# Load order at the start, block 1's inputs kept in SBUF, and outputs held back to stand beside scores, in a memory-augmented transformer with an MLP mixer

## The chip, the cores and the metric

The kernel runs on one core of a Trainium2 chip. The metric is the device time of one execution in microseconds (us), lower is better. A profile comes from one execution, in most runs one of those that are timed. Runs were made in jobs, each with its own runs of the kernel before: the first pair, then three jobs of experiments, of which the first two ran on one chip and the last on another.

Names of engines: PE is the tensor engine, PEld its weight loads, DVE the vector engine, ACT the scalar engine, POOL the gpsimd engine, SP the engine that issues most transfers.

## The reference, cut to what matters

```python
x = A_x                                   # 2048 tokens x 1024, bf16
xn = _layernorm(x)
return x + _A_ref(xn, mem0, Wq, Wk, Wv, Wo, 32) + _B_ref(xn, w1, w2, w3, w4)

# _A_ref: attention in 64 segments of 32 tokens, each with 8 memory rows, 32 heads of 128
#   scores = q k^T * scale; p = softmax(masked scores); o = (p v) Wo
#   the first 8 rows of o are the next segment's memory
# _B_ref: h = gelu(layernorm(x) @ w1); four column groups of h shifted by -1, +1, -2, +2 tokens
#   x1 = x + shifted @ w2; x1 + gelu(layernorm(x1) @ w3) @ w4
```

## The kernel before: the parts that matter

The kernel runs the mixer and the MLP first and the attention afterwards. Its matmul stream is written out by hand. Three places are touched by the change.

The start loads tiles of x (256 KB each) and quarters of w1 (512 KB each) on one queue, SP's. I call them x0, x1, ... and q0 to q3. The first tile is normalized on DVE, transposed on PE and copied by ACT; then 16 matmuls follow for each quarter of w1, as the quarters land.

```python
load_x(0)
load_x(1)
for c in range(4):
    nc.sync.dma_start(w1_sb[:, 2*c:2*c+2, :], w1_v[:, 2*c:2*c+2, :])
    if c == 1:
        load_x(2)
for n in range(3, 7):
    load_x(n)
...
norm_stats(0)
norm_stats(1, 0)          # first half of tile 1's statistics, ahead of tile 0's scaling on DVE
norm2_of(0)
tr(0, 0, True); tr(0, 1, True)
norm_stats(1, 1)
```

Attention works through 5 blocks of 12 to 14 segments. A block's tokens and memory rows, transposed, are gathered in `hTb`. Block 0's are filled straight into SBUF; those of blocks 1 to 4 are filled into a staging tile, written to DRAM, and read back later.

```python
if 1 <= hg < 5:
    hTs = abig.tile(...)                       # staging
    nc.gpsimd.memset(hTs[:], 0.0)
    fill(hTs, tl, lambda j, b=b: xT[:, j])     # DVE copies
    nc.gpsimd.dma_start(hT_d[b][:], hTs[:]...)
```

In attention the big projection matmuls are interrupted by small groups of four: scores (S) and outputs (O). `tick` runs after each projection and issues what is due. An output becomes due 10 us (12 in block 0) after its scores, on the kernel's own count of time. In between, P, the normalized scores, is made on ACT and DVE and transposed by a transfer on SP's queue.

```python
def tick(us, blocked=None):
    clock[0] += us
    load_some(1)
    done = set()
    for item in list(smalls):
        due, kind, fn = item
        if due <= clock[0] and kind != blocked and kind[0] not in done and not (kind[0] == "S" and flying[0] >= 5):
            smalls.remove(item)
            flying[0] += 1 if kind[0] == "S" else -1
            done.add(kind[0])
            clock[0] += fn()
...
smalls.append((clock[0] + (12.0 if gi_ == 0 else 10.0), ("O", gi_), o_item))
```

## Time and profile before

| what | value |
|---|---|
| time, median of the first 3 runs | 1512.88 us (1511.96 to 1513.14) |
| span of the profiled execution | 1511.0 us |
| PE busy | 1499.8 us |
| start of the matmuls of w1's third quarter | 11.32 us |
| first matmul of the attention's projections | 756.06 us |

From the page of the kernel before: the span, the busy time of the engines, the shares of the chain that ended last, and the three costliest PE groups (busy us, mean ns of one, idle us before them).

```profile
span 1511.0 us, 24305 instructions
PE 1499.8 (99%) x9778; PEld 804.0 (53%) x9850; DVE 544.6 (36%) x1136; ACT 504.6 (33%) x1144; POOL 178.9 (12%) x248
...
DMA packets 303539, 274.11 MB, mean 181 GB/s; under 512 B 153926, under 2 KB 270184, under 8 KB 303424
...
PE 98%; DMA 1%; issue 0%; SPq 0%; DVE 0%
...
L655 PE MATMUL ps<-hTb,wt 128*128 128x396 bf16 (+2 forms) x2528 | 495.9, 343 | 0.0
L594 PE MATMUL ps<-wt,xT 128*128 128x512 bf16 x1003 | 220.1, 379 | 1.1
L713 PE MATMUL pso<-wo_sb,oX 128*128 128x512 bf16 (+1 forms) x972 | 209.1, 372 | 1.1
```

PE is the limit. The idle 1.1 us of two groups fit missing records, not waits. The waits view of the kernel before, PE alone, in us in total, times, longest:

```profile
PE ps L307 <- DMA w_sb<-in_B_w_dram: 1.7, 3, 1.0
PE warm L334 <- DVE wz L328: 1.4, 1, 1.4
PE psO L694 <- DMA PT<-Pn: 0.5, 1, 0.5
```

Besides the warm-up there are three waits at the start for w1 and one for a transposed P. The timeline of PE at the start of the kernel before shows the three (start us, duration, engine, line, operation, operands, count, and in brackets the idle time before and what ended it). L307 is w1's matmuls, 16 for each quarter; L294 is the transposes.

```profile
6.53 0.96 PE L294 MATMUL ps<-c_ident_sb,xn 128*128 128x128 bf16 x8
7.96 1.07 PE L307 MATMUL ps<-xn2T,w_sb 128*128 128x128 bf16 x16 [0.47 <-DMA w_sb<-in_B_w_dram]
9.28 1.07 PE L307 MATMUL ps<-xn2T,w_sb 128*128 128x128 bf16 x16 [0.26 <-DMA w_sb<-in_B_w_dram]
11.32 1.07 PE L307 MATMUL ps<-xn2T,w_sb 128*128 128x128 bf16 x16 [0.97 <-DMA w_sb<-in_B_w_dram]
12.23 0.61 PE L294 MATMUL ps<-c_ident_sb,xn 128*128 128x128 bf16 x8
```

In attention, the timeline of PE of the kernel before shows what a pair of small groups costs: from 848.97 to 849.33 us, 0.36 us for eight matmuls of 99 columns, with no idle time on either side.

```profile
848.97 0.34 PE L694 MATMUL psO<-PT,V 99*128 99x99 bf16 x4
849.15 0.34 PE L670 MATMUL psS<-KT,QT 128*128 128x99 bf16 x4
849.33 0.84 PE L655 MATMUL ps<-hTb,wt 128*128 128x403 bf16 x4
```

A matmul's duration in the profile (343 ns in the group above) overlaps the next one's. What counts for the span is the distance between starts: 99 columns come to about 44 ns each, 396 columns to 167.5 ns.

### The profile page before, as it was taken

To read this page: it belongs to the slowest core of one execution; us is meant where nothing else is said; L and a number is where in the kernel's file an instruction comes from. 1 tells how busy PE (TensorE), PEld (TensorE's weight loads), DVE (VectorE), ACT (ScalarE), POOL (GpSimd) and SP (SyncE) were. 2 spreads that over 40 slices of the span, in tenths; PEclk is the share of its full clock that TensorE was granted. 3 is DMA by queue.
4 is the path that set the end of the run, shared out by engine and by line. 5 is a ranking of instruction groups with operands and counts; after the bars stand their busy time and mean duration, and the time that the engine had idled before them with its cause. 6 is when DMAs were issued, how large, how long until landed. Compare 5 with 4: busy or idle time off the path is not lost.

```text
span 1511.0 us, 24305 instructions
## 1 busy us (share of the span) xinstructions
PE 1499.8 (99%) x9778; PEld 804.0 (53%) x9850; DVE 544.6 (36%) x1136; ACT 504.6 (33%) x1144; POOL 178.9 (12%) x248
## 2 busy tenths in 40 slices
PE   9999999999999999999999999999999999999998
PEld 7844444445444444444456645664665455545555
DVE  8383230100020122222246624661564166516641
ACT  6533203013012011111156614650663266416630
POOL 5231020211111231100000000001000100010001
PEclk9999999999999999999999999999999999999999
DMA  8699752453345887632389957992998299918811
GB/s 292 150 265 315 228 168 89 146 202 104 137 149 151 203 261 258 218 121 82 128 216 257 244 128 171 245 252 69 245 243 206 71 227 224 219 60 199 216 49 51
DMA packets 303539, 274.11 MB, mean 181 GB/s; under 512 B 153926, under 2 KB 270184, under 8 KB 303424
## 3 DMA queue, kind: packets, MB, share of 16 engines
q1 hardware_dynamic: 281248, 189.92, 50.1%
q0 software_dynamic: 22032, 82.54, 15.9%
q8 instruction: 79, 1.29, 0.4%
q14 instruction: 36, 0.29, 0.1%
q10 hardware_dynamic: 144, 0.07, 0.0%
HBM read 190.93 MB, written 46.14 MB: 157 GB/s over the span
## 4 chain that ended last, share of the span: by engine, by line
PE 98%; DMA 1%; issue 0%; SPq 0%; DVE 0%
PE ps L655 30%; PE pso L713 15%; PE ps L594 15%; PE ps L536 13%; PE ps L562 13%; PE ps L394 4%; PE ps L317 3%; PE psO L694 2%; PE psS L670 2%; PE ps L849 1%; PE ps L486 1%; DMA w_sb<-in_B_w_dram 1%; DMA PT<-Pn 1%; PE gps L465 0%; PE ps L451 0%
## 5 line engine op out<-in xcount | busy, mean ns | idle before, releaser
L655 PE MATMUL ps<-hTb,wt 128*128 128x396 bf16 (+2 forms) x2528 | 495.9, 343 | 0.0
L655 PEld LDWEIGHTS <-wt 128*128 128x128 bf16 x2528 | 232.7, 98 | 164.9 <-DMA wt<-in_A_Wq_dram 0.4
L594 PE MATMUL ps<-wt,xT 128*128 128x512 bf16 x1003 | 220.1, 379 | 1.1
L713 PE MATMUL pso<-wo_sb,oX 128*128 128x512 bf16 (+1 forms) x972 | 209.1, 372 | 1.1
L536 PE MATMUL ps<-xn3T,w_sb 128*128 128x512 bf16 x896 | 196.2, 379 | 0.0
L562 PE MATMUL ps<-w_sb,h3T 128*128 128x512 bf16 x873 | 194.3, 379 | 1.2
L594 PEld LDWEIGHTS <-xT 128*128 128x128 bf16 x1024 | 100.1, 98 | 120.9
L537 ACT ACTIVATE h3T<-ps 128x512 bf16<-128x512 f32 x112 | 66.8, 597 | 290.4 <-PE ps L536 289.5
L713 PEld LDWEIGHTS <-oX 128*128 128x128 bf16 x992 | 96.0, 98 | 106.6
L657 ACT CAST KT<-ps 128x462 bf16<-128x462 f32 (+2 forms) x160 | 81.7, 511 | 190.0 <-PE ps L655 185.9
L562 PEld LDWEIGHTS <-h3T 128*128 128x128 bf16 x896 | 86.9, 98 | 103.4
L536 PEld LDWEIGHTS <-w_sb 128*128 128x128 bf16 x896 | 86.5, 98 | 102.1
L676 DVE TENSOR_REDUCE sums<-sm 99x4 f32<-99x396 f32 (+2 forms) x176 | 97.6, 555 | 112.9 <-ACT sm L674 112.9
L659 ACT ACTIVATE QT<-ps 128x462 bf16<-128x462 f32 (+2 forms) x160 | 83.8, 524 | 112.6 <-PE ps L655 98.7
L596 ACT CAST Vs<-ps 128x512 bf16<-128x512 f32 x64 | 37.4, 585 | 233.2 <-PE ps L594 175.0
L672 DVE TENSOR_TENSOR sm<-psS,c_mask_reg_sb 99x396 f32<-99x396 f32 x152 | 86.7, 570 | 74.6 <-PE psS L670 74.5
L674 ACT ACTIVATE sm<-sm 99x396 f32<-99x396 f32 (+2 forms) x176 | 92.7, 527 | 57.7 <-DVE sm L672 53.5
L600 DVE CAST Vs<-ps 128x512 bf16<-128x512 f32 x64 | 44.3, 692 | 170.0 <-PE ps L594 160.4
L682 DVE TENSOR_TENSOR Pn<-sm,rs 99x396 bf16<-99x396 f32 (+2 forms) x176 | 98.9, 562 | 7.2 <-DMA PT<-Pn 1.1
L720 POOL DMA_DIRECT2D out_dram<-ot x30 | 16.4, 545 | 699.4 <-DVE ot L719 693.5
L563 DVE TENSOR_TENSOR R<-ps,R 128x512 f32<-128x512 f32 x32 | 21.9, 690 | 180.1 <-PE ps L562 166.2
L719 DVE TENSOR_TENSOR ot<-pso,Rt 128x512 bf16<-128x512 f32 (+1 forms) x33 | 22.2, 675 | 168.5 <-PE pso L713 164.5
(122 smaller groups left out, 1063.0 us busy)
## 6 DMA issues: line engine op xcount, KB each, us to landing
wt<-in_A_Wq_dram SPq DMA_DIRECT2D x76, 512.0 KB
wt<-in_A_Wk_dram SPq DMA_DIRECT2D x76, 512.0 KB
wt<-in_A_Wv_dram POOLq DMA_DIRECT2D x24, 1024.0 KB, 6.9
V_scratch<-Vs SPq DMA_DIRECT2D x32, 512.0 KB
V<-V_scratch SPq DMA_DIRECT2D x40, 384.0 KB
R_scratch<-x POOLq DMA_DIRECT2D x16, 512.0 KB, 4.0
R<-R_scratch SPq DMA_DIRECT2D x16, 512.0 KB
R_scratch<-R POOLq DMA_DIRECT2D x16, 512.0 KB, 3.1
```

What stands on the lines that cost most here:

```text
L536: nc.tensor.matmul(ps[:].rearrange("p (n t) -> p n t", t=P), w3_sb[:, k, f * P:(f + 1) * P], xn3T[tb][:, :, k, :], start=(k == 0), stop=(k ...
L537: nc.scalar.activation(h3T[:, f, :], ps[:], ACTF.Gelu_apprx_tanh)
L562: nc.tensor.matmul(ps[:], h3T[:, f, j * P:(j + 1) * P], w4_sb[:, f, ch * 512:(ch + 1) * 512], start=(f == 0), stop=(f == FT - 1))
L594: nc.tensor.matmul(ps[:], xT[:, m4 * 4 + j, k, :], wv[:, k, :], start=(k == 0), stop=(k == KT - 1))
L655: nc.tensor.matmul(ps[:, :nb], w[:, k, hh * P:(hh + 1) * P], B["hT"][:, k, :nb], start=(k == 0), stop=(k == KT - 1))
L657: nc.scalar.copy(dst[:, hh, :], ps[:, :nb])
L659: nc.scalar.mul(dst[:, hh, :], ps[:, :nb], scale)
L672: nc.vector.tensor_tensor(sm[:T, :, :T], S3, t["mask"][:].unsqueeze(1).to_broadcast((T, 4, T)), op=ALU.add)
L674: nc.scalar.activation(e[:T, :, :T], sm[:T, :, :T], ACTF.Exp, scale=LN2)
L676: nc.vector.tensor_reduce(ss, e[:T, :, :T], axis=AX.X, op=ALU.add)
L682: nc.vector.tensor_tensor(Pn[:T, :, :T], e[:T, :, :T], rs[:T, :].unsqueeze(2).to_broadcast((T, 4, T)), op=ALU.mult)
L713: nc.tensor.matmul(self.ps[:, :self.w], self.oX[0][:, h, self.oX[1] + self.gl * P:self.oX[1] + (self.gl + 1) * P], wo_sb[:, h, self.cc], s ...
```

## The change

The intent: start w1's matmuls sooner, spare block 1's inputs the way through DRAM, and interrupt the projections less often, by letting an output wait (at most 2.5 us on the kernel's count) until the next scores go out.

```diff
-                    load_x(0)
-                    load_x(1)
+                    load_x(0)
                     for c in range(4):
                         nc.sync.dma_start(w1_sb[:, 2 * c:2 * c + 2, :], w1_v[:, 2 * c:2 * c + 2, :])
-                        if c == 1:
-                            load_x(2)
+                        if c < 2:
+                            load_x(1 + c)
...
                     norm_stats(0)
-                    norm_stats(1, 0)
                     norm2_of(0)
                     tr(0, 0, True)
                     tr(0, 1, True)
-                    norm_stats(1, 1)
+                    norm_stats(1)
...
-                if 1 <= hg < 5:
+                if hg < 2:
+                    tl, nb = tiles_of(hg)
+                    hTb01.append(early.tile([P, KT, 416 + 48 * hg], BF16, tag=f"hTb{hg}", name=f"hTb{hg}"))
+                    fill(hTb01[hg], tl, lambda j: xT[:, j])
+                elif hg < 5:
...
-            for item in list(smalls):
+            ready = [i for i in smalls if i[0] <= clock[0] and i[1] != blocked]
+            paired = any(k[0] == "S" for _, k, _ in ready) and flying[0] < 5 or not any(k[0] == "S" for _, k, _ in smalls)
+            for item in ready:
                 due, kind, fn = item
+                if kind[0] == "O" and not paired and clock[0] < due + 2.5:
+                    continue
```

More of the change, by code (lines that the diff above doesn't have):

```diff
@@ L112 @@
     xn_v = xn_d.rearrange("(n p) d -> p n d", p=P)
-    hT_d = {b: tc.dram_tile([P, KT * c], BF16, name=f"hT{b}_scratch") for b, c in ((1, 416), (2, 416), (3, 464), (4, 464))}
+    hT_d = {b: tc.dram_tile([P, KT * c], BF16, name=f"hT{b}_scratch") for b, c in ((2, 416), (3, 464), (4, 464))}
     V_d = tc.dram_tile([S, H * DH], BF16, name="V_scratch")
@@ L580 @@
             wo_sb = abig.tile([P, H, D], BF16)
+            hTb01 = []
             pns = [abig.tile([112, 4, P], BF16, name=f"Pn{i}") for i in range(3)]
@@ L618 @@
                         nc.sync.dma_start(w[:], src[:, :, 512:1024])
-                if hg == 0:
-                    tl, nb = tiles_of(0)
-                    hTb0 = early.tile([P, KT, 416], BF16, tag="hTb0")
-                    fill(hTb0, tl, lambda j: xT[:, j])
             vctx.close()
@@ L632, in block_setup @@
             ntok = sum(t["ntok"] for t in tl)
-            if b == 0:
-                hTb = hTb0
+            if b < 2:
+                hTb = hTb01[b]
             else:
```

## The prediction

> **What bounds the kernel now.** The tensor engine (PE) is busy 1499.8 of 1511.0 us (page, part 1), is 98% of the chain that ended last (part 4), at a granted clock of 1.00; the waits view gives PE only 1.7 us on w1's quarters at the start, 1.4 us before the warm-up and 0.5 us on a transposed P. Busy is not yet peak, so I took start-to-start distances from the trace. The Trainium skill ("TensorE: Matmul & The Clock Gate", section "Wait — 56ns, not 53.3ns?") gives N / 2.4 GHz plus about 2.5 ns for a warm matmul of N columns. The trace agrees almost everywhere: eight projections of 396 columns take 1.34 us, 167.5 ns each. Distances above that, leaving out those that fit a missing record, sum to about 4 us after the warm-up. So a change that removes no matmul can win some 4 us (0.3%).
>
> **Block 1's inputs in SBUF.** Removes one memset on POOL, one 0.85 MB write (near 559 us) and one read back (647 us, landed in 8.4 us, first used over 200 us later). PE waits for neither. Its ten DVE copies (0.18 to 0.36 us each) stay; they may move earlier, as block 0's did (DVE sat 11.3 us waiting for x's transposes near 485 to 497 us). That can delay evictions of the MLP's second product, but four PSUM tiles of 6.05 us each give slack. Gain on PE: 0.
>
> **x tiles between w1's quarters.** On one queue x0, x1, q0, q1, x2, q2 becomes x0, q0, x1, q1, x2, q2. q0 lands one x tile earlier (about 0.7 us), but q1 and q2 have the same bytes before them as before. The waits ending at 7.96 us (0.65 us), 9.28 us (0.42 us) and 11.32 us (1.14 us) are in series: the first shrinks, the next grows by as much, and PE still stands until q2 lands at 11.3 us. x1 lands later (near 7.9 us), so the second tile's normalized rows come near 11.2 us instead of 9.26 us, which the transposes at 12.2 us just allow. Gain 0, at worst a loss of 0.5 us.
>
> **Outputs held back.** Four score matmuls take 0.18 us on PE, as do four output matmuls, alone or as a pair (848.97 to 849.33 us), so interrupting the projections costs nothing measurable: 0 to 2 ns a change. Before, 73 of 176 output groups stand beside a score group in the trace; replaying the issue rule on paper gives about 145 after. Some 70 fewer interruptions are below 0.3 us. Outputs come up to 2.5 us later after their transposed P: the one 0.63 us wait at 799.4 us should go, perhaps 0.13 us at 1405 us. Scores keep their places.
>
> **Sum.** 1512.88 − 0.7 = about 1512.2 us; 8 times in 10 within 1510.4 to 1513.7. Faster by over 2%: 0.01; same: 0.98; slower: 0.01.
>
> **What would show it.** Right: PE busy within 2 us of 1499.8; part 5's means unchanged; waits for w1 again about 1.7 us, with the third quarter's matmuls starting near 11.3 us; about 145 output groups beside scores, still 0.18 us per group; no wait of outputs on P near 800 us; 1.7 MB less traffic. Wrong: third quarter's matmuls a microsecond earlier (the queue is not simply in order), groups shorter or longer in pairs, new PE waits for PSUM near 500 us or on P.
>
> **What would make it wrong.** A collision on the transposes' queue, copies placed so badly on DVE that PE runs out of PSUM tiles, or x1 landing so late that it holds the first transposes.

## The result, and the profile after

The changed kernel took 1510.90 us (median of 6 runs, 1510.73 to 1511.99), the kernel before in the same rounds and the earlier ones 1513.01 us (6 runs, 1511.96 to 1513.98). The ratio is 0.9988, with a 95% interval of 0.9975 to 1.0001. Ratios here are the mean time of one kernel's runs over that of the other's in the same rounds, so not quite the ratio of the medians. By the 2% measure the two are the same; the difference, about 2 us, is at the edge of what the runs separate, and it is the profile that tells what it is made of.

From the page of the changed kernel, the lines that answer to those shown before:

```profile
span 1509.0 us, 24273 instructions
PE 1499.1 (99%) x9778; PEld 804.6 (53%) x9850; DVE 544.6 (36%) x1136; ACT 504.0 (33%) x1144; POOL 175.0 (12%) x245
...
DMA packets 303251, 272.41 MB, mean 181 GB/s; under 512 B 153894, under 2 KB 270152, under 8 KB 303136
...
L654 PE MATMUL ps<-hTb,wt 128*128 128x396 bf16 (+2 forms) x2528 | 484.8, 342 | 0.0
L593 PE MATMUL ps<-wt,xT 128*128 128x512 bf16 x1003 | 220.1, 379 | 1.1
L712 PE MATMUL pso<-wo_sb,oX 128*128 128x512 bf16 (+1 forms) x972 | 208.5, 372 | 1.1
```

The number of matmuls and their mean durations are unchanged, and 1.70 MB of traffic are gone. The 11 us less on the projections are no saving. Before each break, the last projection's duration of 343 ns counts in full, though the next matmul starts 167 ns after it; with 72 breaks fewer (207 instead of 279 in the traces) an estimated 72 x 0.17 = 12 us of overlap are no longer counted to this group (e_outs below, which has the same 207 breaks, shows the same 484.8 us). PE as a whole is busy 0.7 us less. This is a trap in reading busy times group by group.

The waits of PE in the changed kernel, without the warm-up's 1.4 us:

```profile
PE ps L306 <- DMA w_sb<-in_B_w_dram: 0.3, 1, 0.3
PE ps L306 <- ACT xn2T L296: 0.2, 1, 0.2
PE psO L693 <- DMA PT<-Pn: 0.2, 1, 0.2
```

And its timeline of PE at the start (L306 is w1's matmuls):

```profile
7.45 1.95 PE L306 MATMUL ps<-xn2T,w_sb 128*128 128x128 bf16 x32 [0.24 <-ACT xn2T L296]
9.71 1.07 PE L306 MATMUL ps<-xn2T,w_sb 128*128 128x128 bf16 x16 [0.32 <-DMA w_sb<-in_B_w_dram]
10.62 0.61 PE L293 MATMUL ps<-c_ident_sb,xn 128*128 128x128 bf16 x8
11.08 1.07 PE L306 MATMUL ps<-xn2T,w_sb 128*128 128x128 bf16 x16
```

The first two quarters now run without a break, 32 matmuls from 7.45 us, and the third starts at 9.71 instead of 11.32 us. The mixer's second stage (its first matmul with w2) starts at 67.47 instead of 69.06 us: 1.59 us of the gain of 2.0 us in the span lie here. Everything from there to the attention takes equally long, 687.00 us in both.

The rest, 0.5 us, lies in attention. The stretch from its first projection to the last matmul takes 750.34 instead of 750.84 us. To see what it is made of, I set each PE start against the start before it plus N / 2.4 GHz + 2.5 ns (N is the number of columns; the formula is the one that the prediction cites), and called the excess before an output group a wait on P (these sums are a little larger than those of the waits view). That gives 0.79 us before and 0.52 us after, and a break of 0.19 us between projections at 791.9 us that is gone.

The DVE copies for block 1 were indeed moved ahead, from near 557 us to between 495.4 and 509.2 us. In the view of the tile `hTb` in the changed kernel, DVE's idle time for x's transposes is:

```profile
DMA xT<-xn_scratch: 17.2, 6
```

It was 11.3 us in 3 waits before. One eviction of the MLP's second product, at 509.22 us, had to stand behind them. No wait of PE came of it, as the prediction had argued.

### The profile page after: what moved, and what is told of

Read it like the earlier page. It is cut to its first block, busy times and chain, and to the rows that moved or that the text cites. A ratio compares the mean times of both kernels' runs of the same rounds, so it can differ in the third digit from the quotient of the medians.

```text
span 1509.0 us, 24273 instructions
## 1 busy us (share of the span) xinstructions
PE 1499.1 (99%) x9778; PEld 804.6 (53%) x9850; DVE 544.6 (36%) x1136; ACT 504.0 (33%) x1144; POOL 175.0 (12%) x245
## 2 busy tenths in 40 slices
DMA packets 303251, 272.41 MB, mean 181 GB/s; under 512 B 153894, under 2 KB 270152, under 8 KB 303136
## 4 chain that ended last, share of the span: by engine, by line
PE 98%; DMA 1%; issue 0%; SPq 0%; DVE 0%
PE ps L654 30%; PE pso L712 15%; PE ps L593 15%; PE ps L534 13%; PE ps L560 13%; PE ps L392 4%; PE ps L316 3%; PE psO L693 2%; PE psS L669 2%; PE ps L852 1%; PE ps L484 1%; DMA PT<-Pn 1%; PE gps L463 0%; PE ps L449 0%; DMA w_sb<-in_B_w_dram 0%
## 5 line engine op out<-in xcount | busy, mean ns | idle before, releaser
L654 PE MATMUL ps<-hTb,wt 128*128 128x396 bf16 (+2 forms) x2528 | 484.8, 342 | 0.0
L654 PEld LDWEIGHTS <-wt 128*128 128x128 bf16 x2528 | 236.8, 98 | 175.4
```

Source lines behind the costliest of these rows:

```text
L654: nc.tensor.matmul(ps[:, :nb], w[:, k, hh * P:(hh + 1) * P], B["hT"][:, k, :nb], start=(k == 0), stop=(k == KT - 1))
```

## The experiments

Two questions were open. Why does the third quarter land 1.6 us sooner, when the same bytes are ahead of it in the queue? And what, if anything, does the holding back of outputs gain? My theories: T, the order of the loads itself moves the landing; W, held outputs gain only because P has more time to land. Rivals: R, the start differs by chance; P, standing beside scores makes the groups cheaper for PE (this "rival P" has only its letter in common with the matrix P); A, less traffic helps. A second pair, X and Q, came up later and is stated with h_qq.

All numbers in one table; the order of rows is that of the runs. "q2" is the start of the third quarter's matmuls, "stage 2" the first matmul with w2, "stretch" the attention from its first projection to the last matmul, "on P" the sum of waits on P in it, all from the traces by start times and in us. Times are medians, with the kernel before's of the same job behind; a dash marks a single run.

| run | q2 | stage 2 | stretch | on P | time | before | ratio, 95% interval |
|---|---|---|---|---|---|---|---|
| kernel before | 11.32 | 69.06 | 750.84 | 0.79 | | | |
| changed kernel | 9.71 | 67.47 | 750.34 | 0.52 | 1510.90 | 1513.01 | 0.9988 (0.9975 to 1.0001) |
| e_order | 10.30 | 68.06 | 752.64 | 2.25 | 1513.38 | 1514.89 | 0.9984 (0.9966 to 1.0002) |
| e_outs | 11.23 | 68.96 | 750.56 | 0.74 | 1512.49 | 1514.89 | 0.9980 (0.9962 to 0.9997) |
| e_sbuf | 11.30 | 69.05 | 751.77 | 1.93 | 1513.44 | 1514.89 | 0.9988 (0.9971 to 1.0006) |
| e_noorder | 11.54 | 69.27 | 750.71 | 0.91 | 1512.92 | 1514.89 | 0.9988 (0.9968 to 1.0007) |
| b_again | 10.98 | 68.73 | 749.86 | 0.00 | 1511.63 | 1512.42 | - |
| a_again | 10.14 | 67.88 | 749.86 | 0.04 | 1511.20 | 1512.42 | 0.9991 (0.9978 to 1.0005) |
| e_later | 11.05 | 68.79 | 749.84 | 0.00 | 1512.58 | 1512.42 | 1.0000 (0.9986 to 1.0014) |
| e_sooner | 11.36 | 69.10 | 755.12 | 5.29 | 1517.24 | 1512.42 | 1.0027 (1.0011 to 1.0042) |
| h_qq | 10.15 | 68.18 | 749.82 | 0.00 | 1510.92 | 1513.09 | - |
| h_xx | 11.07 | 68.83 | 749.95 | 0.00 | 1511.70 | 1513.09 | - |
| s_held | 10.96 | 68.70 | 751.73 | 1.92 | 1513.88 | 1513.09 | 1.0008 (0.9992 to 1.0023) |
| h_best | 9.55 | 68.10 | 750.74 | 0.92 | 1510.91 | 1513.09 | 0.9986 (0.9973 to 1.0000) |

The first job of experiments (e_order to e_noorder) was a noisy one: the kernel before itself ran from 1512.40 to 1520.62 us in it, with a median about 2 us above those of the other jobs. Ratios there are of little use, and the traces decide.

### e_order: the start alone

```diff
 # kernel before, with the change's load order and norm_stats(1) in one piece; nothing else
```

> Kernel before with the new load order and the undivided statistics of tile 1 alone. Theory T (the order of the loads moves the landing of w1's quarters): the third quarter's matmuls start near 9.7 us as in the changed kernel, PE's waits for w1 sum to about 0.3 us, and the time is about 1.6 us under before. Rival R (the start of the loads differs from run to run or build to build, whatever their order): the third quarter's matmuls start anywhere between 9.7 and 11.3 us and the time does not follow the order.

The third quarter's matmuls started at 10.30 us: between the two, nearer the changed kernel, but later than I had said (9.7). The wait for w1 was 0.8 us, not 0.3. The line of PE's timeline:

```profile
10.30 1.07 PE L306 MATMUL ps<-xn2T,w_sb 128*128 128x128 bf16 x16 [0.79 <-DMA w_sb<-in_B_w_dram]
```

Against e_sbuf of the same job, which has the old order, the second stage started 0.98 us sooner. The order matters; the gain of 1.59 us in the first pair of profiles was a large instance of it. The time was not told apart from before (the interval reaches 1.0002); besides the noise of the job, the profiled run met 2.25 us of waits on P, and one of 0.4 us for a weight tile at 791 us.

### e_outs: holding back alone

```diff
 # kernel before, with the change's ready / paired / continue lines in tick; nothing else
```

> Kernel before with the outputs held back alone. Theory T: head as before (third quarter near 11.3 us), the 0.63 us wait of outputs on P near 799 us shrinks to about 0.4 us and the 0.19 us gap near 792 us goes: time 0.4 to 0.5 us under before. Rival P (pairs are cheaper for PE): more than 1 us under before, with groups shorter than 0.175 us.

The head was as before. The wait near 799 us was 0.49 us, and the break near 792 us was absent. The groups took the 0.18 us they had taken. The measured ratio says 3 us less, which rival P had foretold, but the slow runs of before in this job can make it; the trace accounts for far less (a stretch of 750.56 against 750.84 us in the first profile).

### e_sbuf: block 1's inputs alone

```diff
 # changed kernel, with the start and tick put back as before
```

> Kernel before with block 1's inputs kept in SBUF alone. Theory T: time within 0.3 us of before, head as before (third quarter near 11.3 us), 1.7 MB less traffic. Rival A (less traffic helps block 0's loads): the waits near 792 and 799 us shrink and the time falls by about 0.45 us.

The traffic fell by 1.70 MB, to 272.41 MB, and the head stayed (11.30 us). The wait near 799 us was 0.41 us and the break near 792 us was absent, which rival A had foretold; but the waits on P summed to 1.93 us, with one of 0.70 us at 986.7 us (the waits view puts it down to ACT; the last landing before it is that of a transpose, at 986.56 us), and the unchanged kernel showed neither wait nor break in its second profile. So these small waits come and go without any change in the traffic, and the part gained nothing that the runs can show.

### e_noorder: all but the start

```diff
 # changed kernel, with load order and norm_stats put back as before
```

> Changed kernel with the loads and statistics at the start put back as before. Theory T: 1.6 us of the gain of 2.1 us are lost, third quarter near 11.3 us, about 0.5 us under before. Rival R: the start lands anywhere, and the kernel may be as fast as the changed one.

The head lost what it had gained: 11.54 us for the third quarter, 69.27 us for the second stage, 1.8 us later than in the changed kernel. Theory T stands, rival R is weak.

### b_again and a_again: both kernels profiled a second time

> Kernel before, unchanged, profiled a second time. If the order of the loads decides the start, the third quarter's matmuls start at 11.2 to 11.6 us again; if the start is chance, they may start near 9.7 us. PE's waits of outputs on P after 756 us: 0.9 us in the first profile of this kernel, 1.9 and 2.8 us in the two experiments that issue outputs as it does; expected between 0.5 and 3 us.

> Changed kernel, unchanged, profiled a second time. If the order decides the start, the third quarter's matmuls start at 9.6 to 10.4 us; if it is chance, anywhere up to 11.5 us. Waits of outputs on P after 756 us between 0.4 and 1.0 us. Time about 2 us under before.

The head came out as T wants: 10.98 and 10.14 us, the second stage at 68.73 and 67.88 us, a difference of 0.84 us this time. In this job neither kernel waited on P (0.00 and 0.04 us), below what I had expected for both, and the changed kernel was faster by 1.2 us in the medians instead of 2. That makes it the cleanest test of rival P. In the trace of before, 73 of 176 output groups stand beside scores, in the changed one 145, and the stretch of 750 us takes 749.86 us in both. Pairing by itself gains nothing on PE. The windows view of PE over this stretch, first b_again, then a_again (window, length, busy time and records, clock, DMA):

```profile
755.70:1505.60 749.90, 749.90 (x5285) 1.00 0.72 181
```

```profile
754.80:1504.70 749.90, 749.90 (x5285) 1.00 0.74 181
```

PE is not idle anywhere in it.

### e_later and e_sooner: outputs later or sooner, without pairing

```diff
-smalls.append((clock[0] + (12.0 if gi_ == 0 else 10.0), ("O", gi_), o_item))
+smalls.append((clock[0] + (13.5 if gi_ == 0 else 11.5), ("O", gi_), o_item))   # e_later
+smalls.append((clock[0] + (11.0 if gi_ == 0 else 9.0), ("O", gi_), o_item))    # e_sooner
```

> Kernel before with the outputs due 1.5 us later (13.5 and 11.5 us after their scores) and no pairing rule. Theory W (the rule helps because outputs come later after their transposed P, whose transfer sometimes lands late): waits of outputs on P after 756 us sum to at most 0.7 us and the stretch from the first projection to the last matmul takes about 750.5 us, as with the rule. Rival P (standing beside scores is what helps): waits as without the rule (0.9 to 2.8 us), stretch 751 to 752.6 us.

> Kernel before with the outputs due 1 us sooner (11 and 9 us after their scores). Theory W: the waits of outputs on P after 756 us grow to 4 us or more, and the time by about 3 us or more over before. Rival P: within 1 us of before.

e_later had no waits on P, but neither had the kernel before in the same job, so it tells W and P not apart; its time was that of before. e_sooner did: one microsecond less brought 5.29 us of waits and a ratio of 1.0027, 4.1 us. It speaks against rival P as well: 112 of its 176 output groups stand beside scores, more than the 73 before, and it is slower. The waits view of PE in e_sooner, without the warm-up and the start:

```profile
PE psO L694 <- DMA PT<-Pn: 4.2, 4, 2.2
PE psO L694 <- DMA V<-Vmem_scratch: 0.2, 1, 0.2
```

The two largest in its timeline of PE:

```profile
1085.06 0.34 PE L694 MATMUL psO<-PT,V 99*128 99x99 bf16 x4 [1.20 <-DMA PT<-Pn]
1085.24 0.34 PE L670 MATMUL psS<-KT,QT 128*128 128x99 bf16 x4
1085.41 2.84 PE L655 MATMUL ps<-hTb,wt 128*128 128x396 bf16 x16
1090.44 0.35 PE L694 MATMUL psO<-PT,V 99*128 99x99 bf16 x4 [2.18 <-DMA PT<-Pn]
```

Both outputs stand directly before scores, in pairs, and wait all the same: what decides is P. The second one's P is made by DVE at 1080.05 us, and its way from there goes through this stretch (timeline of e_sooner, DVE's and SP's lines):

```profile
1079.21 1.13 SPq L739 DMA_DIRECT2D wt<-in_A_Wk_dram  x1
...
1080.05 0.57 DVE L682 TENSOR_TENSOR Pn<-sm,rs 99x396 bf16<-99x396 f32 x1
...
1080.40 1.03 SPq L645 DMA_DIRECT2D V<-V_scratch  x1
...
1081.47 0.36 SPq L649 DMA_DIRECT2D V<-Vmem_scratch  x1
...
1081.94 4.90 SPq L685 DMA_TRANSPOSE PT<-Pn  x2
```

P is ready at 1080.62 us, but SP issues the transpose (the first of the two) at 1081.94 us, after the values of the next stage, and it lands just before 1090.44 us, some 8 us later, with a weight load of 512 KB and the values' 384 KB ahead of it on the same queue. That these loads make it late is what the queue suggests; no run here took them away, so it is not shown.

### s_held: the rule put on top of e_sooner

```diff
 # e_sooner, with the change's ready / paired / continue lines in tick
```

> Kernel before with the outputs due 1 us sooner (11 and 9 us), as in the run before, and the rule that holds them back. Replaying the issue rules gives outputs 1.3 us later after their scores on average than without the rule, with the earliest as early. Theory W: waits of outputs on P after 756 us fall from 5.3 us to between 1 and 3.5 us, and the time lies 2 us or more under that of the run without the rule. Rival P: no change in the waits.

The waits on P were 1.92 us instead of 5.29, and the ratio to before 1.0008 instead of 1.0027, 2.9 us less (two jobs on two chips, each against its own runs of before). The two intervals overlap, so the times alone do not settle it; with the waits, one profile of each, they say that the rule shields PE from a late P, as W says. How much that is worth with the real delays depends on the job: over the profiles without the rule at 12 and 10 us the waits on P are 0.79, 2.25, 1.93 and 0.00 us, those with it 0.52, 0.74, 0.91 and 0.04 us, and in the three kernels with further load orders 0.00 (h_qq), 0.00 (h_xx) and 0.92 us (h_best). The means are 1.24 and 0.45 us: the right sign, from few profiles.

### h_qq and h_xx: which part of the load order

```diff
 # changed kernel, loads in another order; in both the same bytes stand ahead of q2
-x0 q0 x1 q1 x2 q2 q3
+x0 q0 q1 x1 x2 q2 q3     # h_qq
+x0 x1 q0 x2 q1 q2 q3     # h_xx
```

> Changed kernel with the loads in the order x0, q0, q1, x1, x2, q2, q3 (two w1 quarters back to back, the same bytes before q2). Theory X (what slows the old order is that x0 and x1 both stand before the first quarter): third quarter's matmuls start at 9.6 to 10.4 us, as in the changed kernel. Rival Q (what slows it is q0 and q1 back to back): 11.0 us or later.

> Changed kernel with the loads in the order x0, x1, q0, x2, q1, q2, q3 (two x tiles first, the first quarters apart, the same bytes before q2). Theory X: third quarter's matmuls start at 11.0 us or later, as in the kernel before. Rival Q: 9.6 to 10.4 us.

The timelines of PE: first h_qq, then h_xx (L308 is w1's matmuls).

```profile
7.51 1.95 PE L308 MATMUL ps<-xn2T,w_sb 128*128 128x128 bf16 x32
10.15 1.07 PE L308 MATMUL ps<-xn2T,w_sb 128*128 128x128 bf16 x16 [0.69 <-DMA w_sb<-in_B_w_dram]
```

```profile
7.77 1.07 PE L308 MATMUL ps<-xn2T,w_sb 128*128 128x128 bf16 x16 [0.41 <-ACT xn2T L298]
9.73 1.07 PE L308 MATMUL ps<-xn2T,w_sb 128*128 128x128 bf16 x16 [0.90 <-DMA w_sb<-in_B_w_dram]
11.07 1.07 PE L308 MATMUL ps<-xn2T,w_sb 128*128 128x128 bf16 x16 [0.28 <-DMA w_sb<-in_B_w_dram]
```

Theory X holds. With q0 right after x0, q2's matmuls start at 10.15 us even with two quarters back to back; with x1 ahead of q0, at 11.07 us even with the quarters apart. Over all runs, the nine traces with x1 ahead of q0 start them at 10.96 to 11.54 us, the four with q0 right after x0 and the same bytes ahead of q2 at 9.71 to 10.30 us. The two ranges do not touch, so it is not chance. Nor is it the other edit at the start, the statistics of tile 1 in one piece: h_xx keeps that edit, and is as late as the kernel before.

How this comes about is seen in part. The DMA records of the traces (2 KB packets, a median of 84 ns each) hold a slow spell, with packets of 250 to 1000 ns, at the start of w1's bytes. In the kernel before it lies from 3.7 to 6.2 us, after most of x0 and x1; in the changed kernel from 2.2 to 3.6 us, where it overlaps x0's own packets. By bytes, the end of q2 has landed at 9.65 us before and 9.05 us after: 0.6 us. But PE is released at 11.32 and 9.71 us, so in the old order the last byte to arrive is late against the count by some 1.7 us, in the new one by 0.7 us (over all runs, 1.1 to 1.9 us in the nine traces and 0.7 to 1.3 us in the four).

The Trainium skill ("DMA: Bandwidth & Descriptors", section "Why a DMA increments its semaphore by 16 and not by 1") says that a transfer is spread over up to 16 engines "that finish independently" and counts as landed only when all have. The traces agree. Each load has 16 semaphore updates, which I read as the landings of its shares. In the kernel before, those of q0 run from 5.37 us over a median of 5.99 to 7.91 us, and those of q2 from 9.47 over 9.92 to 11.28 us. In the changed kernel they run from 4.54 to 5.19 us and from 9.14 to 9.67 us. In all nine traces with x1 ahead of q0, the last share of q0 lands 1.9 to 2.7 us after the first, and the last of q2 follows 3.3 to 3.4 us after it, as if the share that fell behind in q0 never caught up. In the four others q0's shares land within 0.2 to 1.1 us; shares that fall behind appear later and cost less. So PE waits for q2's latest shares and not for the queue as a whole. The updates do not name the engine, so that it is the same one throughout is an inference. Why w1's first bytes are slow stays open.

### h_best: x2 behind all of w1

```diff
-x0 q0 x1 q1 x2 q2 q3
+x0 q0 x1 q1 q2 q3 x2
```

> Changed kernel with x2 behind all of w1's quarters: x0, q0, x1, q1, q2, q3, x2. Theory: the third and fourth quarter land one x tile (0.68 us) sooner, the fourth quarter's matmuls start at 10.5 to 10.9 us instead of 11.1 to 11.7 us, and the second stage starts about 0.5 us sooner, unless x2 comes too late for the third tile's transposes, which then stand in for the wait. Time 0 to 0.6 us under the changed kernel: 1.5 to 2.5 us under before.

The third quarter came at 9.55 us and the fourth at 10.91 us, as hoped, but the second stage started at 68.10 us, no sooner than in the changed kernel (67.47 and 67.88). x2's statistics began only at 11.56 us, and the third tile's transposes held PE. The timelines of h_best, DVE and PE:

```profile
11.56 0.69 DVE L261 BATCH_NORM_STATS2 st<-xt 128x6 f32<-128x512 bf16 x1 [1.77 <-DMA xt<-in_A_x_dram]
...
14.18 0.55 DVE L276 TENSOR_SCALAR xn<-xt,mv,rr 128x1024 bf16<-128x1024 bf16 x1 [0.24 <-POOL rr L267]
```

```profile
14.79 0.40 PE L295 MATMUL ps<-c_ident_sb,xn 128*128 128x128 bf16 x4
```

These transposes started 0.30 us later than the matmul before them allowed; two further breaks of 0.18 and 0.33 us followed at 32.9 and 33.6 us. The time, 1510.91 us, is that of the changed kernel. No version was found that beats it.

## Why the prediction was right, and where it was not

- **The bound.** Right. PE busy was 1499.1 us after 1499.8, and no group of matmuls became faster. The possible gain of about 4 us was the right scale: some 2 us were had.
- **Block 1's inputs.** Right: no gain could be shown, traffic down by 1.70 MB, the copies moved ahead, no new wait of PE.
- **The start.** Wrong. The step that failed is "q1 and q2 have the same bytes before them as before", taken to mean that q2 lands at 11.3 us. In its place: the landing depends on what the queue carries first, because PE waits for the last share of each load, and with x1 ahead of q0 some of q0's shares fell up to 2.7 us behind. The second stage started 1.59 us sooner in the first pair of profiles and 0.84 us in the second. Averaged, the eight traces with the old order start it at 68.96 us and the three with the new one at 67.80 us, a gain of 1.15 us. The side step was wrong in the same direction: I expected the second tile's normalized rows near 11.2 us, and they were begun at 9.21 us, because x1, too, came sooner (its last share at 5.96 us) than the 7.9 us at which I had put it. The prediction named the sign to look for (third quarter's matmuls a microsecond earlier, "the queue is not simply in order"), and it appeared; what it shows is less a queue out of order than shares that fall behind in a slow spell, whose place and cost depend on the order.
- **Pairs.** Right: 145 output groups beside scores, 0.18 us a group as before, and a stretch of 749.86 us with 73 pairs or with 145 when nothing waits on P.
- **Waits on P.** Right in mechanism, mis-sized. The term was 0.63 us plus perhaps 0.13 us, read from one profile. In the first profile after, the wait near 800 us had not gone, as forecast, but shrunk to 0.38 us. Over the profiles, the waits on P that the rule can act on are anything from 0 to 2.25 us from job to job, and the difference of the means is about 0.8 us, from four profiles and seven.
- **The sum.** 1512.2 us was forecast, 1510.9 us measured, inside the range of 1510.4 to 1513.7 us. The missing 1.3 us are about the term of the start that was put at 0. That the number still fell inside is owed to the width of the range, not to this term.

## What to carry to other kernels

Where one engine streams at its own rate, as PE did here, regrouping its instructions gained nothing; look at what it waits for, and measure start-to-start distances, not busy times. At the very start of a kernel, do not reckon landings from bytes alone: try putting the first weight piece directly behind the input that is needed first, and measure it on the chip, since the same bytes in another order came 1 us sooner here. A wait read from one profile can be worth anything from nothing to a few times its size in another run, as here (0.79 us, then 0.00 to 2.25); before judging a change that gives it slack, take the slack away on purpose and see what the wait does.

## What the Trainium skill lacked or had wrong

- "TensorE: Matmul & The Clock Gate", section "Back-to-back issue gap", gives sustained distances of about 131 ns for N = 512 and 81 ns for N = 128 for streams of weight load and matmul. The streams here keep a median of 216 ns and 56 ns, with a weight load before every matmul: the formula N / 2.4 GHz + 2.5 ns, which that section calls the isolated one, is the one that holds. (The section of the same page that the prediction names has it right.)
- The same section says that at small N the formula is too low because it has no share for weight loads. Groups of four matmuls with 99 columns, each with its own weights, cost 0.175 to 0.18 us, and the change between them and projections 0 to 2 ns in the median: no share for weight loads is to be seen.
- "DMA: Bandwidth & Descriptors" says nothing of a slow spell in the first microseconds of a kernel: packets of 2 KB took 250 to 1000 ns instead of 84 ns in a spell whose place depends on the order of the loads, worth 0.8 to 1.6 us here. In it, the shares of one load landed up to 2.7 us apart.
- No page says how much landing times differ from run to run: the same kernel, before, waited 0.79 us on transposed P in one job and 0.00 us in another.
